# A gated mix of two linear-attention layers on one core: the first weights loaded by column groups on one queue, and a new order of the same operations

## The chip, the cores and the metric

One core of one Trainium2 chip runs the whole kernel. The metric is device time in microseconds of one execution. The kernel before was run three times; beside these one execution was taken with the hardware profiler, and all rows come from that one.

## The reference

The input x has 2048 tokens of 640 features; there are 32 heads of 20 features. Two attentions read the same x and are mixed by a gate per token.

```python
g = sigmoid((x * gate_w).sum(-1, keepdims=True))
# A: linear attention with softmax features
q, k, v = split(x @ wqkv)
phi(t) = concat(softmax(t @ w_phi), softmax(-(t @ w_phi)))       # 20 + 20 features
o_A = (phi(q) @ (phi(k).T @ v)) / (phi(q) @ phi(k).sum(tokens) + 1e-6)
# B: four segments of 512 tokens
p = softmax(q k.T / sqrt(20) + causal mask)                      # in the segment
a_mem = phi2(q) @ M / (phi2(q) @ z + 1e-6)                       # M, z: sums over the segments before
o_B = sigmoid(beta) * a_mem + (1 - sigmoid(beta)) * (p @ v)
out = g * (o_A @ wo_A) + (1 - g) * (o_B @ wo_B)
```

phi2(t) is t + 1 where t > 0 and exp(t) elsewhere. All tensors are bf16.

## The kernel before, in words

The program is a graph of 1317 operations. The functions of class GatedMix make them, in order of definition; three tables at the end of the file then say everything about their order. ORDER lists the operations' numbers in one sequence, and each engine executes its own operations in that sequence; ENGINE picks an engine for each operation that can run on more than one (an eviction from PSUM on ScalarE or VectorE, an elementwise step on VectorE or GpSimd); PLACE picks the PSUM banks and SBUF slots. The three came from a search outside the file, on a model of the chip. Semaphore waits follow from the reads and writes that each operation declares (emit, from L156 on). An engine is in order: an operation that waits holds all behind it, and this holds for SP's list of DMAs too.

The stages, by function:

- setup (L400): loads, weight layouts and masks. x is loaded as xT, features on partitions, by four transposing DMAs, x0 to x3, of 512 tokens each (L382). B's q and k weights are loaded into the staging tiles stq and stk (800 KB each, L386) and copied from there into WB (L439), where each head's 20 columns lie at a partition group of 32: for each of five column chunks c and for q and k, WB0 copies 80 columns and WB1 48. A's w_phi is folded into A's q and k weights (fuse, L500) from the transposed weights wkT and wqT; that gives WkA and WqA. "warm" is twelve matmuls on zeros (L427).
- b_proj(n) (L509) for each segment n: ten projections qkproj (five chunks by q and k; five matmuls of 512 columns each, L516); an eviction qk_ev for each chunk; four DMAs relw that write the rows 20 to 31 of each partition group to DRAM and four DMAs relr that read them back as head groups 5 to 7 of tile qk (numbered relr#0 to #15 over the segments); four value projections vproj (ten matmuls of 320 or 321 columns, L536 and L537; column 640 is the gate, loaded by GpSimd's DMA gw) with their eviction.
- b_pair (L644): scores of head groups. Three bursts per group (QKn.j#i, L628), each followed by two exps on ScalarE (L639) and a mask on GpSimd (L641); then PV (L673), and its division on VectorE (L680, L684).
- b_mem and b_ret: the memory. k is transposed by DMA (ktr), phi2 is applied, the sums M are kept; b_ret reads the memory for a segment (matmuls mr, L604, then mre, mrr, mrm on VectorE, L610 to L612).
- a_k(t) for each of 16 token tiles: pkA and vA (ten matmuls of 320 columns each, L702), two exps, sums and normalization (Anorm). a_kv sums phi(k) v in PSUM (kv) and phi(k) over tokens in tile acc by 64 adds, the "chain" (L763), which VectorE and GpSimd share: adds of one half follow one another whichever engine has them.
- a_fin: the matmuls zmm on acc (L775) and the scaled tile KV1, which all of A's outputs need.
- a_q(S) for each segment: pqA (L806), exps, ssum, whose result goes through DRAM by four DMAs rw (640 runs of 256 bytes each) and one DMA rd; then U (L851).
- final(t): out tiles, twenty matmuls of 320 columns each (L878), eviction and store.

The head before, in the order of each queue. SP: x1, WvA, x0, wkT, x3, wqT. ScalarE: the loads WvB, stq, stk, then its copies. GpSimd: gw, beta, wphi, then masks and copies. TensorE: warm, two value projections, qkproj0#0 and #1, one value projection, a first burst, then value projections, fuses and token projections mixed with the other eight qkproj0, of which the last, #9, stands 44th in TensorE's list. Around the second half, SP's list reads rw#0 to rw#3, relr#11, A_wo, relr#9, rd#0, and TensorE's burst QK2.2#2, which needs relr#8 to #11, follows.

Of the kernel before, what the change touches and what calls it, by code (L numbers as in the profile page):

```python
# [13 lines left out]
D = 640  # L14
# [3 lines left out]
NCH = 5  # L18
# [226 lines left out]
class GatedMix(Graph):  # L245
# [154 lines left out]
    def setup(self):  # L400
        ins, op = self.ins, self.op
        x2d = ins["A_x"].rearrange("b s d -> (b s) d")
        wqkv = ins["A_wqkv"]
        wsrc = lambda w: w.rearrange("(c p) n -> p c n", p=128)
        xT = self.xT
        self.dma("sp", "x0", xT[:, :, 0:LSEG], x2d[0:LSEG, :], W=[(xT, 0)], transpose=True)
        self.dma("act", "stq", self.stq[:, :, :], wsrc(ins["B_wq"]), W=[(self.stq, "*")])
        self.dma("act", "stk", self.stk[:, :, :], wsrc(ins["B_wk"]), W=[(self.stk, "*")])
        self.dma("act", "WvB", self.WvB[:, :, 0:D], wsrc(ins["B_wv"]), W=[(self.WvB, "w")])
# [21 lines left out]
        for c in range(NCH):  # L431
            for w in range(2):
                Wv = lambda w=w, c=c: self.WB[:, w, :, 128 * c:128 * (c + 1)].rearrange("p k (b r) -> p k b r", r=32)
                for part, (c0, n, r0, r1) in enumerate(((80 * c, 80, 0, DH), (400 + 48 * c, 48, DH, 32))):
                    o = op(("dve", "act", "pool"), f"WB{part}", None, R=[(st[w], "*")], W=[(self.WB, (w, c, part))])

                    def fn(e, o=o, Wv=Wv, w=w, c0=c0, n=n, r0=r0, r1=r1):
                        a, b = Wv()[:, :, :, r0:r1], st[w][:, :, c0:c0 + n].rearrange("p k (b r) -> p k b r", r=r1 - r0)
                        return e.activation(a, b, ACT.Copy) if o.stream == "act" else e.tensor_copy(a, b)  # L439
                    o.fn = fn  # L440
# [512 lines left out]
"""  # L953
ENGINE = "".join("""
210002211012121211121101010000110110101011110111101110011110111100011011000111011111111001010000111010101000001101011101011100010101101111110010001011
00100000101011111000110100101001100000001111000000001101011110101111111111100111000110001111111000
""".split())
PLACE = """
# [64 lines left out]
```

## Time and profile before

| | us |
|---|---|
| three runs | 339.05, 339.27, 341.5 |
| median | 339.27 |
| the profiled execution, its own time | 338.27 |
| its span, first to last instruction | 336.2 |
| TensorE's mean granted clock in it | 0.949 of full |

The profiled execution's own time is 2.07 longer than its span. Engines are named in the rows as PE (TensorE's matmuls), PEld (its weight loads), DVE (VectorE), ACT (ScalarE), POOL (GpSimd) and SP; a q behind the name (SPq) is that engine's issuing of DMAs. In a timeline a row gives start, duration, engine, line, operation, out<-in, count, and in brackets the idle time before it with what ended that. A row with xN is a run of N instructions of one form.

### The profile page before, as it was taken

The numbers are of one execution on the slowest core, as the hardware profiler recorded it, in microseconds if no ns is written. First come the engines' busy times: TensorE is split into PE (matmuls) and PEld (weight loads), VectorE is DVE, ScalarE is ACT, GpSimd is POOL, SyncE is SP. The second block draws the span as 40 slices with busy tenths as digits, with TensorE's granted clock in tenths as the row PEclk, the third lists the DMA queues.
The fourth block names the chain that finished last, engine by engine and source line by source line (L and its number), as shares of the span: only waits on it lengthen the run. The fifth ranks groups of instructions, "written<-read, shape, count | busy, mean of one in ns | idle before, by whom it ended". The sixth has DMA issues, their size and how long they took to land.

```text
span 336.2 us, 8681 instructions
## 1 busy us (share of the span) xinstructions
PE 298.2 (89%) x3726; PEld 188.0 (56%) x3726; DVE 243.9 (73%) x400; ACT 238.6 (71%) x276; POOL 196.8 (59%) x191
## 2 busy tenths in 40 slices
PE   4279999989899798998999698699989899799996
PEld 1136755655546665667576363346466667467874
DVE  3144778689999879988989986658486794554661
ACT  1228888878779679988879285688987876676402
POOL 6132147668899579998999781550445915514260
PEclk9789999999899899999999597869999999899999
DMA  8995005514201462024003313603479537612363
GB/s 196 272 238 120 0 2 86 95 41 91 20 2 31 76 100 60 16 18 67 16 2 99 75 23 95 189 3 81 94 188 186 110 80 134 173 55 69 80 99 117
DMA packets 68901, 29.42 MB, mean 88 GB/s; under 512 B 57952, under 2 KB 66944, under 8 KB 68864
## 3 DMA queue, kind: packets, MB, share of 16 engines
q1 hardware_dynamic: 66800, 26.39, 36.8%
q10 hardware_dynamic: 1968, 2.46, 2.6%
q8 instruction: 29, 0.48, 0.6%
q0 software_dynamic: 96, 0.04, 0.3%
q14 instruction: 8, 0.07, 0.1%
HBM read 9.54 MB, written 7.21 MB: 50 GB/s over the span
## 4 chain that ended last, share of the span: by engine, by line
PE 51%; DVE 23%; DMA 10%; ACT 4%; issue 4%; SPq 4%; POOL 3%; ACTq 0%; DVEq 0%; POOLq 0%
PE ps L878 9%; PE ps L516 8%; PE ps L702 7%; PE ps L806 6%; PE ps L673 6%; DVE acc L763 5%; PE ps L628 4%; DMA xT<-in_A_x_dram 4%; PE ps L851 3%; DVE E L724 2%; SPq L386 2%; DMA qk<-scr 2%; ACT exA L639 2%; SPq L382 2%; POOL acc L763 2%
## 5 line engine op out<-in xcount | busy, mean ns | idle before, releaser
L639 ACT ACTIVATE exA<-ps 128x1024 bf16<-128x1024 f32 x128 | 124.3, 1024 | 30.8 <-PE ps L628 30.2
L641 POOL TENSOR_SCALAR_AFFINE_SELECT exA<-exA 128x1024 bf16<-128x1024 bf16 (+1 forms) x64 | 60.3, 950 | 74.2 <-ACT exA L639 73.2
L763 POOL TENSOR_TENSOR acc<-acc,E 64x640 bf16<-64x640 bf16 x29 | 46.3, 1600 | 10.4 <-DMA acc<-acc 5.3
L516 PE MATMUL ps<-xT,WB 128*128 128x512 bf16 x200 | 50.3, 392 | 0.4 <-DVE qk L395 0.4
L628 PE MATMUL ps<-qk 20*128 20x384 bf16 (+3 forms) x512 | 32.8, 309 | 12.9 <-DVE aM L612 3.8
L673 PEld LDWEIGHTS ps<-v1B,exA 128*128 128x128 bf16 x1024 | 35.8, 96 | 5.5 <-issue 1.3
L673 PE MATMUL ps<-v1B,exA 128*128 128x21 bf16 x1024 | 37.2, 173 | 1.3 <-POOL exA L641 0.6
L639 ACT ACTIVATE exC<-ps 128x1024 bf16<-128x1024 f32 x32 | 31.3, 1025 | 8.8 <-PE ps L628 8.8
L516 PEld LDWEIGHTS ps<-xT,WB 128*128 128x128 bf16 x200 | 18.5, 101 | 23.2 <-issue 5.8
L536 PE MATMUL ps<-WvB,xT 128*128 128x320 bf16 x80 | 23.5, 311 | 8.3 <-DMA xT<-in_A_x_dram 8.1
L641 POOL TENSOR_SCALAR_AFFINE_SELECT exC<-exC 128x1024 bf16<-128x1024 bf16 x16 | 19.8, 1238 | 15.0 <-ACT exC L639 14.9
L763 DVE TENSOR_TENSOR acc<-acc,E 64x640 bf16<-64x640 bf16 x33 | 27.6, 846 | 0.9 <-POOL acc L763 0.2
L724 POOL TENSOR_TENSOR E<-E,z 128x640 bf16<-128x640 bf16 x20 | 26.1, 1314 | 3.1 <-DVE z L722 2.7
L806 PE MATMUL ps<-xT,WqA 128*128 128x512 bf16 x100 | 27.7, 424 | 0.2 <-ACT exC L639 0.2
L878 PE MATMUL ps<-Wo,oTA 128*128 128x320 bf16 x160 | 25.5, 310 | 2.1 <-DVE out L395 2.1
L628 PEld LDWEIGHTS ps<-qk 20*128 20x128 bf16 x512 | 9.2, 92 | 32.1 <-issue 12.4
L702 PE MATMUL ps<-WkA,xT 128*128 128x320 bf16 x160 | 25.7, 310 | 1.5 <-DVE qk L395 1.5
L813 ACT ACTIVATE ET<-ps 128x1024 bf16<-128x1024 f32 (+1 forms) x24 | 20.8, 883 | 7.1 <-PE ps L806 5.7
L714 ACT ACTIVATE E<-ps 128x640 bf16<-128x640 f32 x32 | 22.6, 709 | 4.2 <-PE ps L702 3.8
L673 PE MATMUL ps<-v1B,exC 128*128 128x21 bf16 x256 | 24.9, 172 | 0.0
L702 PE MATMUL ps<-WvA,xT 128*128 128x320 bf16 x160 | 24.3, 299 | 0.5 <-ACT exA L639 0.5
L720 DVE TENSOR_REDUCE z<-E 128x64 f32<-128x1280 bf16 x16 | 23.5, 1469 | 1.5 <-ACT E L714 1.5
(115 smaller groups left out, 549.6 us busy)
## 6 DMA issues: line engine op xcount, KB each, us to landing
scq<-rr SPq DMA_DIRECT2D x16, 160.0 KB
sp<-scq SPq DMA_DIRECT2D x4, 640.0 KB, 5.1
out_dram<-out SPq DMA_DIRECT2D x16, 160.0 KB, 3.7
scr<-qk SPq DMA_DIRECT2D x16, 120.0 KB
qk<-scr SPq DMA_DIRECT2D x16, 120.0 KB
WvB<-in_B_wv_dram ACTq DMA_DIRECT2D x1, 800.0 KB, 4.8
stq<-in_B_wq_dram ACTq DMA_DIRECT2D x1, 800.0 KB, 11.0
stk<-in_B_wk_dram ACTq DMA_DIRECT2D x1, 800.0 KB, 13.1
```

The source lines that it names most:

```text
L516: r = e.matmul(self.pf(pt, w, 0, LSEG), lhsT=WB[:, w, kc, 128 * c:128 * (c + 1)], rhs=xT[:, kc, LSEG * n:LSEG * (n + 1)], start=(kc == 0), ...
L536: e.matmul(self.pf(pt, 0, 0, 320), lhsT=l, rhs=self.WvB[:, kc, 0:320], start=(kc == 0), stop=(kc == 4))
L628: r = e.matmul(self.pf(pts[i // 2], i % 2, c0, N), lhsT=qk[32 * i:32 * i + DH, g, 1, 128 * j:128 * (j + 1)], rhs=qk[32 * i:32 * i + DH, g, ...
L639: self.op("act", "exp", lambda e, p=p: e.activation(view(p), self.pbanks(pts[p], 512), ACT.Exp, scale=scale), W=[(pts[p], 0), (t, (key, p))])
L641: self.op("pool", "mask" + str(len(pat)), lambda e: e.affine_select(mv(), mv(), pattern=pat, compare_op=ALU.is_ge, fill=0.0, base=0, chann ...
L673: r = e.matmul(self.pf(pt, 0, 84 * q + 21 * i, 21), lhsT=src(j, i, q), rhs=vt[:, j, head_of(g, i), :], start=(j == 0), stop=(j == q), skip ...
L702: r = e.matmul(self.pf(pt, b, 0, 320), lhsT=l, rhs=W[:, kc, 320 * b:320 * b + 320], start=(kc == 0), stop=(kc == 4))
L720: self.op("dve", "Zred", lambda e: e.tensor_reduce(z[:, :, :].rearrange("p s h -> p (s h)"), E[:, :, :].rearrange("p s (h d) -> p (s h) d" ...
L724: self.op(("pool", "dve"), "Anorm", lambda e, s=s: e.tensor_tensor(Ev(s), Ev(s), z[:, s, :].rearrange("p (h o) -> p h o", o=1).to_broadcas ...
L763: self.op(("dve", "pool"), "chain", lambda e, src=src, s=s, lo=lo: e.tensor_tensor(acc[lo:lo + 64, s, :], acc[lo:lo + 64, s, :], src(), AL ...
L806: r = e.matmul(self.pf(pt, k, 0, LSEG), lhsT=self.WqA[:, kc, 128 * c:128 * (c + 1)], rhs=xT[:, kc, LSEG * S:LSEG * (S + 1)], start=(kc == ...
L878: r = e.matmul(self.pf(pt, b, 0, 320), lhsT=oT[:, c, :], rhs=self.Wo[:, NCH * k + c, 320 * b:320 * b + 320], start=(first and c == 0), sto ...
```

## The change

Three things change.

1. The loads of the head. stq and stk are no longer loaded whole by ScalarE but by SP, in twelve pieces right after x0, in the order q then k, for column groups (chunk 0), (chunks 1, 2), (chunks 3, 4); each group has two pieces, the 80-column and the 48-column part of its chunks, so runs of 160 and 96 bytes for the first group and of 320 and 192 bytes for the others, 640 runs in each piece. WvB is loaded by SP too. A copy into WB now waits for its own piece alone.

```diff
-        self.dma("act", "stq", self.stq[:, :, :], wsrc(ins["B_wq"]), W=[(self.stq, "*")])
-        self.dma("act", "stk", self.stk[:, :, :], wsrc(ins["B_wk"]), W=[(self.stk, "*")])
-        self.dma("act", "WvB", self.WvB[:, :, 0:D], wsrc(ins["B_wv"]), W=[(self.WvB, "w")])
+        for l, (a, b) in enumerate(((0, 1), (1, 3), (3, NCH))):
+            for nm, st in (("B_wq", self.stq), ("B_wk", self.stk)):
+                for k, c0, c1 in ((0, 80 * a, 80 * b), (1, 400 + 48 * a, 400 + 48 * b)):
+                    self.dma("sp", f"st{k}", st[:, :, c0:c1], wsrc(ins[nm])[:, :, c0:c1], W=[(st, (k, l))], noncontig=True)
+        self.dma("sp", "WvB", self.WvB[:, :, 0:D], wsrc(ins["B_wv"]), W=[(self.WvB, "w")])
...
-                    o = op(("dve", "act", "pool"), f"WB{part}", None, R=[(st[w], "*")], W=[(self.WB, (w, c, part))])
+                    o = op(("dve", "act", "pool"), f"WB{part}", None, R=[(st[w], (part, (c + 1) // 2))], W=[(self.WB, (w, c, part))])
```

2. ORDER and PLACE are new throughout (1327 operations; the others are the same ones). The head by queue, read from the new ORDER. SP: x0, the twelve pieces, wkT, WvB, then segment 0's relw#1 and relw#0, WvA, wqT, x1, a ktr, the other relw, relr. GpSimd: six small masks and the loads wphi and beta among them, then masks and four of WB's copies, then gw. TensorE: warm, qkproj0 #0, #1, #2, #5, #3, #4, #8, a burst, qkproj0 #9, #7, the five fuses of WkA, qkproj0#6, a burst, pkA, a burst, the first value projection, then token and value projections mixed with bursts. Later, SP's list reads relr#11, relr#10, A_wo, two ktr, relr#8, rw#3, relr#9, rw#2, rw#1, rw#0, rd#0. Between ssum#0 and QK2.2#2 TensorE has five pqA projections, two mr, three bursts, two PV, a value projection and ssum#1 (before: two qkproj, three value projections, four bursts and a PV).

3. ENGINE is new. Operations per engine, before and after:

| operation | ScalarE | VectorE | GpSimd |
|---|---|---|---|
| chain and its first copy | | 33, 48 | 31, 16 |
| value eviction of B (v_ev) | 7, 0 | 9, 16 | |
| qk eviction | 6, 11 | 14, 9 | |
| Anorm | | 12, 13 | 20, 19 |
| memory added to the output (aMadd) | | 3, 5 | 9, 7 |
| scaling by rd's result (Esc1, Esc2) | | 6, 3 | 6, 9 |
| scaling of U's reciprocal | 2, 7 | 14, 9 | |
| copies into WB | 9, 5 | 4, 11 | 7, 4 |
| fuse eviction | 6, 4 | 4, 6 | |
| vA and out evictions | 16, 14 | 16, 18 | |
| first kv eviction, K1, Mz1, zero fill of qk | 2, 1 | 5, 7 | 4, 3 |

## Rows read from the trace of the kernel before

**Rows 1.** The page: busy time of the engines; TensorE's strip in 40 slices.
```profile
PE 298.2 (89%) x3726; PEld 188.0 (56%) x3726; DVE 243.9 (73%) x400; ACT 238.6 (71%) x276; POOL 196.8 (59%) x191
...
PE   4279999989899798998999698699989899799996
```

**Rows 2.** Windows: length, then busy us (instructions) of each engine, clock, DMA share, GB/s.
```profile
0.00:26.00 26.00, 13.26 (x59) 6.17 (x60) 8.65 (x31) 5.40 (x10) 10.63 (x37) 0.87 1.01 235
26.00:80.00 54.00, 52.93 (x570) 31.86 (x568) 40.74 (x66) 45.96 (x60) 27.26 (x27) 1.00 0.29 57
80.00:205.00 125.00, 112.90 (x1476) 72.22 (x1475) 114.73 (x167) 100.16 (x114) 104.57 (x80) 0.94 0.24 44
205.00:230.00 25.00, 21.51 (x192) 11.01 (x191) 14.95 (x28) 17.41 (x18) 10.71 (x9) 0.83 0.41 110
```

**Rows 3.** Timeline of SP: issues of DMAs in the head and in three later places.
```profile
0.81 4.85 SPq L382 DMA_TRANSPOSE xT<-in_A_x_dram  x1
...
6.60 11.09 SPq L382 DMA_TRANSPOSE xT<-in_A_x_dram  x1
...
24.46 3.73 SPq L382 DMA_TRANSPOSE wqT<-in_A_wqkv_dram  x1
...
178.69 0.41 SPq L386 DMA_DIRECT2D Wo<-in_B_wo_dram  x1
...
237.06 2.68 SPq L386 DMA_DIRECT2D scq<-rr  x4
241.87 0.40 SPq L386 DMA_DIRECT2D sp<-scq  x1
```

**Rows 4.** Timeline of TensorE: the head, and around the stall at 216 us.
```profile
4.69 4.65 PE L427 MATMUL ps<-zero 128*128 128x512 bf16 x12 [4.69 <-DVE zero L421]
...
15.36 0.42 PE L536 MATMUL ps<-WvB,xT 128*128 128x320 bf16 x1 [6.01 <-DMA xT<-in_A_x_dram]
...
21.62 2.32 PE L516 MATMUL ps<-xT,WB 128*128 128x512 bf16 x10
...
26.98 1.52 PE L702 MATMUL ps<-WvA,xT 128*128 128x320 bf16 x10
...
29.73 0.79 PE L500 MATMUL ps<-BD,wkT 128*128 128x140 bf16 x12
...
215.98 0.40 PE L628 MATMUL ps<-qk 20*128 20x256 bf16 x8 [2.97 <-DMA qk<-scr]
...
218.42 2.31 PE L806 MATMUL ps<-xT,WqA 128*128 128x512 bf16 x5 [0.21 <-ACT exC L639]
```

**Rows 5.** Timeline of ScalarE: the first exp.
```profile
25.71 1.02 ACT L639 ACTIVATE exA<-ps 128x1024 bf16<-128x1024 f32 x1 [0.70 <-PE ps L628]
```

**Rows 6.** DMA: the queue's packets from 18 to 22 us; issues, us to landing.
```profile
q1 hardware_dynamic: 3794, 0.96, 106.1%
...
wphi<-in_A_w_phi_dram POOLq DMA_DIRECT2D x1, 25.0 KB, 8.5
WvB<-in_gate_w_dram POOLq DMA_DIRECT2D x1, 1.2 KB, 9.3
...
wqT<-in_A_wqkv_dram SPq DMA_TRANSPOSE x1, 5.7
```

**Rows 7.** Chain of waits in order of time, 196 to 224 us: start, us, what.
```profile
196.70 0.35 PE ps L775 x10
...
209.15 6.79 DMA qk<-scr
```

**Rows 8.** Groups of instructions by line and form: busy us, mean ns | idle before.
```profile
L763 POOL TENSOR_TENSOR acc<-acc,E 64x640 bf16<-64x640 bf16 x29 | 46.3, 1600 | 10.4 <-DMA acc<-acc 5.3 <-DVE E L724 3.0
...
L763 DVE TENSOR_TENSOR acc<-acc,E 64x640 bf16<-64x640 bf16 x33 | 27.6, 846 | 0.9 <-POOL acc L763 0.2
...
L395 DVE CAST qk<-ps 128x1024 bf16<-128x1024 f32 x14 | 17.1, 1219 | 10.3 <-PE ps L516 10.3
...
L395 DVE CAST v1B<-ps 128x640 bf16<-128x640 f32 x9 | 7.4, 827 | 0.3
```

More of the change, by code (lines that the diff above doesn't have):

```diff
@@ L915 @@
 ORDER = """
[37 rows of a table removed]
[37 rows of a table added]
 """
 ENGINE = "".join("""
-210002211012121211121101010000110110101011110111101110011110111100011011000111011111111001010000111010101000001101011101011100010101101111110010001011
-00100000101011111000110100101001100000001111000000001101011110101111111111100111000110001111111000
+002000100101021100221010011011010001011111011101111111010010010111110111011000111101111100001010011101010011000000000001011110010010001100100000001100
+00100001000000110000110101111000001100000000111100001011111101001001110011011111001111001101110001
 """.split())
 PLACE = """
[11 rows of a table removed]
[11 rows of a table added]
 """
```

96 rows, old and new, of tables (ORDER, PLACE) are left out of this document.

## The prediction, made before the changed kernel was run

> **What bounds the kernel now.** I read the page first, then the windows by stage, then SP's and TensorE's timelines of the head, then the chain of waits. On the page TensorE is the busiest engine, busy 89% of the span, and its strip shows where the rest is: three weak slices at the head (4, 2, 7, then 9s) and dents between two thirds and three quarters of the way (6, 8, 6) [rows 1]. The windows say the same in us: until 26 us TensorE is busy 13.26 of 26.00, from 26 to 80 us 52.93 of 54.00, so there it is the bound; from 80 to 205 us VectorE is busy 114.73 of 125.00 and TensorE 112.90, so those two share the limit; from 205 to 230 us neither is full and the clock is 0.83 [rows 2].
>
> The head is bound by loads. SP first issues x1 and WvA, then x0, whose issue alone takes 11.09 us because ACT's three 800 KB loads fill the DMA engines [rows 3]. The warm-up matmuls begin at 4.69 us and last 4.65. The first real matmul starts at 15.36, having waited 6.01 us for xT; the first q and k projections start at 21.62 [rows 4]; the first exp starts at 25.71 [rows 5]. ScalarE needs q and k before it has an exp to do, and q and k come late.
>
> **The change part by part.** I count TensorE's work at the full-clock pace: ten matmuls of 512 columns (two q or k projections) 2.16, from the chain's pace of the 2.32 row less its tail; a token projection (ten of 320 columns) 1.52 with its tail, 1.39 without; a fuse (six matmuls) half of a 0.79 row less tail, 0.31 [rows 4].
>
> *Head loads.* x0 goes first; it starts at 0.81 like x1 before, so SP is free at 5.7 at the latest (4.85 of issue beside three loads; 3.73 for a transpose with little beside it). It lands about 5.7 us after its issue begins, as wqT did [rows 3, 6], at 6.5. Then SP issues twelve pieces. Each has 640 runs, as have the four scq writes whose issue took 2.68 together, 0.67 each; 0.41 for one Wo load, 640 runs too, is the lower end [rows 3]. At 0.67 the last piece is issued at 5.7 + 8.0 = 13.7. A piece lands about 2.1 us after its issue: the read that waited for those four writes went out at 241.87, 2.13 after the last issue ended at 239.74 [rows 3]. The upper end is wphi, 640 short runs, 8.5 us after its issue [rows 6]. Runs as short as 96 to 320 bytes from DRAM don't stand in this trace; the nearest are the transposes' 253-byte packets (3794 for 0.96 MB in 4 us with all engines full), 16.9 ns per packet and engine [rows 6]. At that price 7680 packets on 16 engines take 8.1 us, no more than their issue.
>
> So q's first group (pieces 1 and 2) is there at 5.7 + 1.3 + 2.1 = 9.1, its two copies, a quarter us each by my estimate from the other short copies, end at 9.6, and TensorE starts real work at 9.7 instead of 15.36, 0.4 us after the warm-up ends. Five matmuls took 2.31 at the half level (1.2 GHz) [rows 4]; the clock hadn't risen at 15.36, since a matmul of 320 columns took 0.42, so I take the first two projections at the half level: 4.6, and the other eight 8.6. The later pieces arrive at 10.4, 11.8, 13.1, 14.5 and 15.8 by twos, each ahead of its projection. Two bursts (0.7) and five fuses (1.6) stand among them; wkT, issued at 13.7, lands at 19.4, before its first fuse. In all 9.7 + 15.5 = 25.2. By then TensorE has done 10.8 + 0.7 + 1.6 = 13.1 us of full-clock work. Before, by 25.2 it had done three value projections and two q/k projections: 3 x 1.39 + 2.2 = 6.4. Gain 6.7 us. From there both kernels give TensorE work without a gap, as 26 to 80 us shows for the one before [rows 2]. Ends: with 8.5 us landing everything is 6.4 later and the gain 0.3; with 0.41 per issue and the full clock at once it is about 9.7. I take 6.7, by the nearest rows.
>
> WvB, which ACT issued first thing, now stands behind wkT on SP: issued at 13.7 + 3.7 = 17.4 with its 0.8 MB. Its first use stands behind a token projection and a burst after the 25.2 above, at 27; it costs nothing while these cover it, and wkT's 5.7 would put its landing at 23. GpSimd issues the gate column (gw, the same first use) behind its last weight copy, which waits for piece 12: issued at about 17, and with the 9.3 us that it took before [rows 6], landed at 26.5. That cover is the thinnest; each us past 27 would be a us of the gain. WvA, wqT, x1 now stand behind segment 0's first two relw, which wait for the last qk eviction (some 27 us); with at most 3.7 each to issue and 5.7 to land they are there by 40, and their first uses are 12 token projections' worth of TensorE work later (after 42). No cost; each of them has that cover.
>
> *SP around segment 2's last relr.* Before, QK2.2#2 (segment 2's first burst of a pair that needs relr) waits for relr#9, which SP reaches only behind four rw, relr#11 and A_wo; the chain has 6.79 us of DMA here [rows 7], TensorE is idle 2.97 at 215.98, and two projections behind it run at the half level, at 2.31 each instead of half of that [rows 4], 2.97 + 2.31 = 5.3 in all. Now relr#9 is behind a single rw and the load of A_wo was issued before; between that rw's release (ssum#0) and the burst stand 10.6 us of TensorE work where 8.9 stood. The wait should go. What is late next is the memory read's VectorE chain, which also holds TensorE here. So 0 to 5.3; I take half, 2.6.
>
> *Engines.* VectorE gets 13 of the chain's adds (0.846 each, 11.0), 7 value evictions (0.827, 5.8), and gives up 5 qk evictions (1.219, 6.1) [rows 8]; the dozen other moves, at one to three operations each, I estimate at 3 more. So VectorE +13.7, GpSimd -13 x 1.6 = -20.8 and a little [rows 8], ScalarE about -3. Most of the adds fall before zmm (at 196.7 [rows 7]), in the stretch where VectorE has 125.00 - 114.73 = 10.3 us free [rows 2]; with the 6.7 us that the head gives, 17 us are there for some 12. The ends are 0 and +13.7; I take +2, near the free time's end, since GpSimd's slow adds, after which VectorE's adds of the same chain waited, go too.
>
> *The rest of the order* is permuted everywhere. No row prices that; its bounds are 12.1 us either way, what TensorE idles from 80 to 205 us (125.00 - 112.90 [rows 2]). I take 0.
>
> Sum: -6.7 - 2.6 + 2.0 = -7.3 on the profiled execution's 338.27: 331.0. That execution is 1.0 under the median of the three runs, 0.3%, less than any term's error; I give 331 for the median too.
>
> **The rivals.**
> 1. *More than the head.* The stall at 216 goes wholly and a third of TensorE's 12.1 idle us between 80 and 205 with it, without a charge for VectorE: -6.7 - 5.3 - 4.0, 322.3. For it: these losses stand in the old order, not in the operations. Against: in an in-order kernel the next late thing takes most of such a gain. 0.11.
> 2. *The head's gain is absorbed.* TensorE is 6.7 us ahead at 25 us, but VectorE, nearly full from 80 us on, reaches zmm no sooner than at 196.7: 338. For it: VectorE's 114.73 of 125.00 [rows 2]. Against: TensorE's 52.93 of 54.00 before it, so an early head moves that whole stretch. 0.17.
> 3. *VectorE becomes the bound, slower.* If it stays at its 92% share with 12 us more before zmm, that stretch takes 12 / 0.92 = 13 longer; less the head's 6.7, +6.3: 345. It decides from the point where zmm comes later than 196.7 + 1. Against: the chain's next operand comes from VectorE itself, so its share can rise. 0.09.
> 4. *The pieces land one after another.* If each piece is issued and landed before the next is served, 0.67 + 2.13 = 2.8 each, the seventh and eighth arrive at 28 and the last at 39; ten projections end near 41 with 13.1 us of work done, where before 22 were done: 9 us lost, 347. Against it: four such DMAs took 4.81 from first issue to the read behind them, not 11.2 [rows 3]. 0.08.
>
> The Trainium skill speaks for the fourth: "DMA: Bandwidth & Descriptors", section "Anatomy of one DMA", gives a fixed cost of about 2 us per DMA plus bytes at 436 GB/s, measured on GpSimd's queue. By it, were the twelve served in turn, they would take 12 x 2.0 + 3.8 = 27.8 us, an estimate, and the last would land near 33. The four writes' 4.81 us [rows 3] say that most of that cost overlaps.
>
> **How the numbers follow.** The forecast has 0.55, the rivals 0.11, 0.17, 0.09 and 0.08. About 1% (3.4 us) is what a measurement of this kernel can tell from no change. Faster by over 1%: forecast and rival 1, 0.66. Within 1%: rival 2, 0.17. Slower: rivals 3 and 4, 0.17. The range runs from rival 1's 322 to 341, past rival 2; it leaves out rivals 3 and 4 and little else.
>
> **What would show it.** Right: first TensorE work at about 9.7 us, first exp near 20 instead of 25.71; TensorE busy over 16 of the first 26 us; SP's pieces 0.6 to 0.8 us apart; no DMA wait before QK2.2#2; zmm at 188 to 192. Wrong: last piece landing after 20 us; zmm at 196 or later with VectorE over 95%; GpSimd idle while VectorE's chain is what the end waits for.

## The result, and the profile after

The changed kernel took 327.71 us (median of 4 runs, 327.3 to 329.87), the kernel before 339.16 beside it (4 runs): ratio 0.9669, 95% interval 0.9599 to 0.9739. Forecast was 331.0 in a range of 322 to 341. The profiled execution has a span of 326.3 us where the one before had 336.2: 9.9 us less. A second set of runs of the same kernel gave 329.25 (6 runs, ratio 0.9669 again, 0.9627 to 0.9711), so the experiments below are set against both medians. One execution of all those reported here, a fourth of the kernel with the new loads under the old order, was slow (369.08 us at a mean granted clock of 0.75) and is left out of that kernel's numbers.

The page, busy time and TensorE's strip, answering to [rows 1]:

```profile
PE 294.8 (90%) x3726; PEld 186.1 (57%) x3726; DVE 243.4 (75%) x425; ACT 236.2 (72%) x270; POOL 173.7 (53%) x172
...
PE   5999999989989599896898769989899999999995
```

The three weak slices at the head (4, 2, 7) are one (5, then 9s). TensorE's sum fell by 3.4 us, so most of the 9.9 is idle time that went. GpSimd lost 23.1 us, and VectorE, which got 25 instructions more, is at 243.4 where it was at 243.9.

The windows, answering to [rows 2], with the same columns:

```profile
0.00:26.00 26.00, 21.56 (x122) 9.37 (x122) 9.97 (x40) 12.08 (x18) 10.98 (x36) 0.93 0.78 153
26.00:80.00 54.00, 51.56 (x664) 32.23 (x664) 48.40 (x79) 47.71 (x56) 30.17 (x28) 1.00 0.45 79
80.00:205.00 125.00, 106.96 (x1329) 67.07 (x1328) 112.72 (x173) 92.58 (x105) 75.48 (x60) 0.93 0.29 59
205.00:230.00 25.00, 23.70 (x400) 15.35 (x398) 19.15 (x37) 21.70 (x25) 14.36 (x12) 1.00 0.61 127
```

In the first 26 us TensorE is busy 21.56 instead of 13.26. From 205 to 230 us the clock is 1.00 instead of 0.83. From 80 to 205 us TensorE is busy 106.96 where it was 112.90, so it idles 18.0 us instead of 12.1: part of what the head won is lost here (below).

SP's timeline of the head, answering to [rows 3]:

```profile
0.81 2.86 SPq L382 DMA_TRANSPOSE xT<-in_A_x_dram  x1
3.73 1.13 SPq L385 DMA_DIRECT2D stq<-in_B_wq_dram  x2
4.91 1.76 SPq L385 DMA_DIRECT2D stk<-in_B_wk_dram  x2
...
10.23 1.18 SPq L385 DMA_DIRECT2D stk<-in_B_wk_dram  x2
11.45 4.16 SPq L382 DMA_TRANSPOSE wkT<-in_A_wqkv_dram  x1
15.65 0.58 SPq L386 DMA_DIRECT2D WvB<-in_B_wv_dram  x1
```

x0 takes 2.86 us to issue, not 4.85, and the twelve pieces go out from 3.73 to 11.41, most of them 0.55 to 0.6 apart. TensorE's timeline, answering to [rows 4], and ScalarE's first exp, answering to [rows 5]:

```profile
1.33 4.53 PE L429 MATMUL ps<-zero 128*128 128x512 bf16 x12 [1.33 <-DVE Mk L448]
7.97 5.10 PE L518 MATMUL ps<-xT,WB 128*128 128x512 bf16 x15 [2.11 <-DVE WB L441]
13.49 4.48 PE L518 MATMUL ps<-xT,WB 128*128 128x512 bf16 x20 [0.42 <-ACT WB L441]
...
211.60 0.40 PE L630 MATMUL ps<-qk 20*128 20x256 bf16 x8
211.93 1.25 PE L518 MATMUL ps<-xT,WB 128*128 128x512 bf16 x5
```

```profile
18.51 1.94 ACT L641 ACTIVATE exA<-ps 128x1024 bf16<-128x1024 f32 x2
```

Real work starts at 7.97 instead of 15.36, and the first exp at 18.51 instead of 25.71. At 211.60 stands QK2.2#2, before at 215.98 behind a wait of 2.97: it waits for nothing now, and the projection behind it takes 1.25 for five matmuls, the full clock, where the two behind it took 2.31 each. The zmm, at 196.70 in [rows 7]:

```profile
189.08 0.41 PE L777 MATMUL ps<-onec,acc 64*128 64x1 bf16 x10 [3.36 <-DVE acc L765]
```

It comes 7.6 us earlier, but not because TensorE is that far ahead. Two windows from the start to the zmm, the kernel before and then the changed one, with the columns of [rows 2]:

```profile
0.00:196.70 196.70, 171.90 (x1972) 105.89 (x1973) 156.47 (x243) 145.02 (x174) 139.12 (x140) 0.95 0.37 75
```

```profile
0.00:189.08 189.08, 166.70 (x1878) 100.50 (x1879) 157.24 (x261) 138.52 (x160) 111.23 (x119) 0.96 0.40 76
```

The new order has 94 fewer matmuls ahead of its zmm, 5.2 us of busy time; only 2.4 of the 7.6 us are idle time saved (24.8 against 22.4). The groups, answering to [rows 8]:

```profile
L765 DVE TENSOR_TENSOR acc<-acc,E 64x640 bf16<-64x640 bf16 x46 | 38.5, 845 | 2.2 <-DMA acc<-acc 1.2
...
L765 POOL TENSOR_TENSOR acc<-acc,E 64x640 bf16<-64x640 bf16 x16 | 23.6, 1476 | 16.3 <-DMA acc<-acc 7.5 <-DVE acc L765 4.4 <-DVE E L726 3.9
```

### The profile page after: what moved, and what is told of

It is laid out like the page before. It is cut to its first block, busy times and chain, and to the rows that moved or that the text cites. A ratio compares the mean times of both kernels' runs of the same rounds, so it can differ in the third digit from the quotient of the medians.

```text
span 326.3 us, 8697 instructions
## 1 busy us (share of the span) xinstructions
PE 294.8 (90%) x3726; PEld 186.1 (57%) x3726; DVE 243.4 (75%) x425; ACT 236.2 (72%) x270; POOL 173.7 (53%) x172
## 4 chain that ended last, share of the span: by engine, by line
PE 51%; DVE 29%; DMA 5%; SPq 4%; ACT 4%; POOL 4%; issue 3%
PE ps L880 11%; DVE acc L765 9%; PE ps L675 7%; PE ps L518 6%; PE ps L808 6%; PE ps L630 5%; PE ps L704 4%; SPq L382 4%; PE ps L853 3%; DVE z L722 3%; PE ps L743 2%; DVE E L726 2%; PE ps L538 2%; ACT exA L641 2%; DMA xT<-in_A_x_dram 2%
## 5 line engine op out<-in xcount | busy, mean ns | idle before, releaser
L643 POOL TENSOR_SCALAR_AFFINE_SELECT exA<-exA 128x512 bf16<-128x512 bf16 (+1 forms) x64 | 61.4, 966 | 73.4 <-ACT exA L641 73.2
L630 PE MATMUL ps<-qk 20*128 20x256 bf16 (+3 forms) x512 | 32.7, 309 | 9.9 <-DVE v1B L395 3.0
L765 DVE TENSOR_TENSOR acc<-acc,E 64x640 bf16<-64x640 bf16 x46 | 38.5, 845 | 2.2 <-DMA acc<-acc 1.2
L765 POOL TENSOR_TENSOR acc<-acc,E 64x640 bf16<-64x640 bf16 x16 | 23.6, 1476 | 16.3 <-DMA acc<-acc 7.5
L808 PE MATMUL ps<-xT,WqA 128*128 128x512 bf16 x100 | 26.1, 404 | 0.8 <-DVE oB L686 0.8
L630 PEld LDWEIGHTS ps<-qk 20*128 20x128 bf16 x512 | 9.2, 92 | 29.5 <-issue 13.7
L880 PE MATMUL ps<-Wo,oTA 128*128 128x320 bf16 x160 | 24.3, 300 | 0.2 <-DMA oTA<-oA 0.2
L643 POOL TENSOR_SCALAR_AFFINE_SELECT exC<-exC 128x1024 bf16<-128x1024 bf16 x16 | 18.9, 1181 | 9.8 <-ACT exC L641 9.6
L880 PE MATMUL ps<-Wo,oTB 128*128 128x320 bf16 x160 | 24.0, 299 | 0.0
```

Source lines behind the costliest of these rows:

```text
L630: r = e.matmul(self.pf(pts[i // 2], i % 2, c0, N), lhsT=qk[32 * i:32 * i + DH, g, 1, 128 * j:128 * (j + 1)], rhs=qk[32 * i:32 * i + DH, g, ...
L643: self.op("pool", "mask" + str(len(pat)), lambda e: e.affine_select(mv(), mv(), pattern=pat, compare_op=ALU.is_ge, fill=0.0, base=0, chann ...
L765: self.op(("dve", "pool"), "chain", lambda e, src=src, s=s, lo=lo: e.tensor_tensor(acc[lo:lo + 64, s, :], acc[lo:lo + 64, s, :], src(), AL ...
L808: r = e.matmul(self.pf(pt, k, 0, LSEG), lhsT=self.WqA[:, kc, 128 * c:128 * (c + 1)], rhs=xT[:, kc, LSEG * S:LSEG * (S + 1)], start=(kc == ...
L880: r = e.matmul(self.pf(pt, b, 0, 320), lhsT=oT[:, c, :], rhs=self.Wo[:, NCH * k + c, 320 * b:320 * b + 320], start=(first and c == 0), sto ...
```

## The experiments

All kernels but one (the new loads under the old order) are the changed one with one edit, of which the lines that matter are shown. Differences are given against 327.71 and 329.25 in turn. The theory: the head's time comes from x0 going first and from column groups, and carries through; the relr stall is a term of its own; the moved adds cost or gain little.

**Whole tiles instead of column groups.** Two loads on SP take the place of the twelve, and each copy into WB waits for its whole tile.

```diff
...
-                    self.dma("sp", f"st{k}", st[:, :, c0:c1], wsrc(ins[nm])[:, :, c0:c1], W=[(st, (k, l))], noncontig=True)
+        self.dma("sp", "stq", self.stq[:, :, :], wsrc(ins["B_wq"]), W=[(self.stq, "*")])
+        self.dma("sp", "stk", self.stk[:, :, :], wsrc(ins["B_wk"]), W=[(self.stk, "*")])
...
```

> The changed kernel, but q's and k's weights come as two whole tiles on SP (x0, q, k, wkT, WvB) and each copy waits for its whole tile. Theory (one queue in order of need gives the head its gain; the column groups only matter if whole tiles arrive later than TensorE can use them): 1.64 MB in long rows needs about 4.5 us at 370 GB/s against about 8 us for the pieces, so q whole lands near 8 us, k near 10.5, first projection at 8 to 9 us instead of 7.97, and SP is free for wkT some 6 us earlier: within 1 us of the changed kernel, 327 to 329. Rival (the column groups are what gives the gain): first projection 3 us or more later, 331 or more.

Measured: 332.76, 5.1 or 3.5 slower (ratio to before 0.9828, 0.9754 to 0.9902). TensorE's timeline of it:

```profile
11.08 11.17 PE L516 MATMUL ps<-xT,WB 128*128 128x512 bf16 x35 [4.45 <-DVE WB L439]
```

The first projection waits for all of wq and starts 3.1 us later. The theory that one long load would do as well was wrong: with this list of SP the groups win, although two whole tiles need far fewer issues. Not all of the 3.1 us need be the tile's length, though: with only two loads ahead of it, wkT is issued from 4.95 us on, beside the two tiles (11.45 in the changed kernel), while the DMA engines are full (a share of 1.14 from 4 to 12 us). No run has whole tiles with a later wkT.

**The old loads under the new order.** ScalarE issues stq, stk and WvB whole, as before; the order and the engines are the new ones, and each copy into WB waits for its whole tile.

```diff
...
-                    self.dma("sp", f"st{k}", st[:, :, c0:c1], wsrc(ins[nm])[:, :, c0:c1], W=[(st, (k, l))], noncontig=True)
-        self.dma("sp", "WvB", self.WvB[:, :, 0:D], wsrc(ins["B_wv"]), W=[(self.WvB, "w")])
+        self.dma("act", "stq", self.stq[:, :, :], wsrc(ins["B_wq"]), W=[(self.stq, "*")])
+        self.dma("act", "stk", self.stk[:, :, :], wsrc(ins["B_wk"]), W=[(self.stk, "*")])
+        self.dma("act", "WvB", self.WvB[:, :, 0:D], wsrc(ins["B_wv"]), W=[(self.WvB, "w")])
...
```

> The changed kernel, but the three head loads are issued by ScalarE as before (WvB, q, k whole) beside SP's x0. Theory (the head's gain comes from loading on one queue in order of need, so that x0 and q don't share the DMA engines with what is needed later): first projection at 12 to 14 us, first exp 4 to 5 us later than in the changed kernel, and the whole 4 to 5 us longer, about 332. Rival (the new order of TensorE's work, projections first, is the gain, whoever loads): within 1.5 us of the changed kernel.

Measured: 336.96 (10 runs), 9.3 or 7.7 slower; ratio to before 0.9956 (0.991 to 1.0002). Its timeline:

```profile
13.68 5.77 PE L516 MATMUL ps<-xT,WB 128*128 128x512 bf16 x15 [7.86 <-DMA xT<-in_A_x_dram]
```

x0, beside three large loads, lands so late that TensorE starts at 13.68. The new order and engines without their loads are worth almost nothing.

**A later head.** wkT and WvB go ahead of x0 in SP's list; nothing else moves.

```diff
+    order = [17, 13] + [a for a in order if a not in (17, 13)]
```

> The changed kernel, but wkT and WvB (1.64 MB) are issued on SP ahead of x0 and the pieces, so that the first projection comes about 5 us later and nothing else changes. Theory (a head that is ahead moves the whole kernel): the end comes later by the same 4 to 5 us, about 332. Rival (the head's gain is absorbed, because VectorE is nearly full from 80 us to zmm): zmm moves by less than 2 us and the end by less than 2 us, 328 to 329.5.

Measured: 335.18, 7.5 or 5.9 slower (0.99, 0.9822 to 0.9977). TensorE's timeline, at the head and at 77 us:

```profile
13.43 3.74 PE L518 MATMUL ps<-xT,WB 128*128 128x512 bf16 x10 [7.01 <-DVE WB L441]
...
77.53 3.79 PE L518 MATMUL ps<-xT,WB 128*128 128x512 bf16 x9 [0.19 <-issue]
...
195.49 0.40 PE L777 MATMUL ps<-onec,acc 64*128 64x1 bf16 x10 [3.36 <-DVE acc L765]
```

The head starts 5.5 us late and zmm is 6.4 late: nothing downstream absorbs a late head in this order. The part above 5.5 is the clock. Against the first profile of the changed kernel the lag is 5.4 until 75 us and 7.1 after nine matmuls at 77.53 that ran at the half level (1.2 GHz), behind a TensorE idle of 0.84; in that first profile ten matmuls behind the same idle took 2.33:

```profile
69.64 0.49 PE L502 MATMUL ps<-BD,wqT 128*128 128x140 bf16 x6 [0.84 <-DVE qk L395]
...
71.86 2.33 PE L518 MATMUL ps<-xT,WB 128*128 128x512 bf16 x10
```

In the second profile of the same, unchanged kernel they took 4.02, at a granted clock of 0.58 (1.00 in the first):

```profile
69.09 0.49 PE L502 MATMUL ps<-BD,wqT 128*128 128x140 bf16 x6 [0.83 <-DVE qk L395]
...
71.31 4.02 PE L518 MATMUL ps<-xT,WB 128*128 128x512 bf16 x10
...
189.45 0.40 PE L777 MATMUL ps<-onec,acc 64*128 64x1 bf16 x10 [3.36 <-DVE acc L765]
```

So whether the clock falls there differs from execution to execution, and it is worth some 1.7 us. Against that second profile zmm is 6.0 late for a head that starts 5.5 late (13.43 against 7.89).

**Pieces, but copies that wait for the whole tile.** Each copy into WB waits for all six pieces of its tile; SP's list stays as it is.

```diff
-                    o = op(("dve", "act", "pool"), f"WB{part}", None, R=[(st[w], (part, (c + 1) // 2))], W=[(self.WB, (w, c, part))])
+                    o = op(("dve", "act", "pool"), f"WB{part}", None, R=[(st[w], (q, l)) for q in range(2) for l in range(3)], W=[(self.WB, (w, c, part))])
...
```

> The changed kernel with its twelve pieces, but every copy into WB waits for all six pieces of its tile, so the groups are loaded and not used. Theory (the grouping pays because TensorE can start on the first group): the first projection starts at 13 to 14 us, when q's last piece lands, 5 to 6 us later than in the changed kernel, and, with the 1.4 us at the end for each us at the head that the late-head run showed, the end is 7 to 9 us later, 335 to 337. Rival (grouping doesn't matter, only the queue's order does): within 1.5 us of the changed kernel.

Measured: 335.19, 7.5 or 5.9 slower (0.9876, 0.9812 to 0.994).

```profile
13.68 4.72 PE L518 MATMUL ps<-xT,WB 128*128 128x512 bf16 x15 [7.24 <-DVE WB L441]
```

The pieces alone lose against two whole tiles (13.68 against 11.08): what cutting gains, it gains because each copy waits for its piece alone.

**The new loads under the old order.** This is the kernel before, its order and engines, with the change's loads; SP issues x1, WvB, x0 and then the pieces. Against the kernel before, beside the loads themselves:

```diff
-    k.replay([int(w) for w in ORDER.split()], [int(w) for w in ENGINE], place)
+    order = [a + 10 if a > 2 else a for a in map(int, ORDER.split()) if a not in (1, 2)]
+    head = [18, 13, 0] + list(range(1, 13))
+    k.replay(head + [a for a in order if a not in head], [int(w) for w in ENGINE], place)
```

> The kernel before with its own order and engines, but with the head's loads all on SP: x1, WvB, x0, the twelve pieces, WvA, wkT and on; each copy waits for its own piece. Theory (the loads are what was won in the head, and a head that is ahead moves any order): the first value projection starts near 9 us instead of 15.36, the first exp near 17 instead of 25.71, the end 5 to 9 us earlier than before, 331 to 335. Rival (only the new order can use the early weights, the old one was searched for late ones): within 2 us of the kernel before.

Measured: 340.4 (median of three runs, 337 to 341.9), ratio to before 1.0014 (0.9922 to 1.0107): no gain. TensorE's timeline:

```profile
10.63 0.30 PE L538 MATMUL ps<-WvB,xT 128*128 128x320 bf16 x1 [1.57 <-issue]
...
20.49 4.45 PE L518 MATMUL ps<-xT,WB 128*128 128x512 bf16 x10 [6.09 <-ACT WB L441]
```

The old order begins with value projections, so x1, WvB and x0 come ahead of the pieces, and the pieces go out from 10.81 on. The first q and k projections start at 20.49, behind an idle of 6.09, and run at the half level; they started at 21.62 before. The first value projection did come earlier (10.63 for 15.36), but TensorE was busy 12.98 of the first 26 us, where it was 13.26 before: in the one arrangement that was tried, the loads give the old order no lead at all. So this run says that they don't pay alone; what a lead would be worth under the old order it doesn't say.

**The relr behind the writes again.** relr#11, A_wo and relr#9 stand behind the four rw, as in the kernel before.

```diff
+    late = [500, 1093, 498]
+    order = [a for a in order if a not in late]
+    i = order.index(1109) + 1
+    k.replay(order[:i] + late + order[i:], [int(w) for w in ENGINE], place)
```

> The changed kernel, but on SP relr#11, the load of A_wo and relr#9 stand behind segment 0's four rw again, as in the kernel before. Forecast's term (the wait before the first burst that needs relr#8 to #11 is worth 0 to 5.3 us, half taken): the burst waits 1 to 4 us for qk from DRAM near 212 us and the end comes 1 to 4 us later, 329 to 332. Rival (TensorE's longer row of work between ssum#0 and that burst covers it, whatever SP's order): no wait, within 1 us of the changed kernel.

Measured: 333.29 (329.77 to 334.4), 5.6 or 4.0 slower (0.9806, 0.9729 to 0.9883).

```profile
216.13 0.61 PE L630 MATMUL ps<-qk 20*128 20x256 bf16 x8 [2.31 <-DMA qk<-scr]
217.07 1.91 PE L518 MATMUL ps<-xT,WB 128*128 128x512 bf16 x4 [0.33 <-issue]
```

The wait is back, 2.31 us of the 2.97 before, and the half clock behind it. zmm came at 190.7, so 1.6 of the loss (1.3 against the second profile) arose ahead of the stall, though nothing there was edited; the other 2.7 to 4.0 us came with the stall.

**x1, WvA and wqT right behind WvB.**

```diff
+    early = [18, 21, 22]
+    order = [a for a in order if a not in early]
+    i = order.index(13) + 1
+    k.replay(order[:i] + early + order[i:], [int(w) for w in ENGINE], place)
```

> The changed kernel, but SP issues x1, WvA and wqT right behind WvB at 16 us, where it is idle until 25.9, and not behind the first two relw. Theory (these three loads are on the chain of waits from 26.6 to 42 us in the changed kernel, though TensorE is busy for all but 2.4 of the 54 us after 26): 0.5 to 2 us faster, 326 to 327. Rival (they have cover, as forecast, and now stand in front of relw and relr, which the segment's second half needs): no change within 1 us or slower by up to 2.

Measured: 327.63 (6 runs, 326.31 to 329.06), ratio 0.9656 (0.9603 to 0.9709): no change. The cover that the forecast gave these late loads was there.

**The chain's adds on the engines of before** (33 on VectorE, 29 on GpSimd, the same adds as before on each).

```diff
-            o.stream = o.engs[e]
+            o.stream = o.engs[int(next(chain)) if o.name == "chain" else e]
```

> The changed kernel with the engines of the 62 chain adds as before the change (33 on VectorE and 29 on GpSimd, not 46 and 16); the sequence is the same. Theory of the forecast (VectorE's extra adds mostly fit its free time and cost about 2 us): 1 to 3 us faster, about 326. Second theory (the moved adds help, since GpSimd's add takes nearly twice as long and the chain's adds follow one another): 2 to 8 us slower, zmm later by as much. No change within 1 us would say that neither engine's share decides.

Measured: 335.03, 7.3 or 5.8 slower (0.9875, 0.9794 to 0.9956), with the same head. Two views show it, TensorE's timeline and, for the second row, GpSimd's:

```profile
71.29 0.49 PE L503 MATMUL ps<-BD,wqT 128*128 128x140 bf16 x6 [3.24 <-DVE qk L396]
...
119.99 0.55 PE L676 MATMUL ps<-v1B,exA 128*128 128x21 bf16 x14 [7.09 <-POOL exC L644]
...
196.74 0.42 PE L778 MATMUL ps<-onec,acc 64*128 64x1 bf16 x10 [6.94 <-DVE acc L766]
```

```profile
107.86 2.03 POOL L766 TENSOR_TENSOR acc<-acc,E 64x640 bf16<-64x640 bf16 x1 [6.91 <-DVE acc L766]
110.65 1.39 POOL L766 TENSOR_TENSOR acc<-acc,E 64x640 bf16<-64x640 bf16 x1 [0.76 <-DVE E L727]
...
113.69 1.39 POOL L766 TENSOR_TENSOR acc<-acc,E 64x640 bf16<-64x640 bf16 x1
...
118.59 1.34 POOL L644 TENSOR_SCALAR_AFFINE_SELECT exC<-exC 128x1024 bf16<-128x1024 bf16 x1
```

GpSimd waits 6.91 us for VectorE's part of the chain, does three adds and the two normalizations and two masks between them, and only then the mask exC for which TensorE waits 7.09. That wait doesn't stand in the changed kernel; the waits at 71 and at zmm were 0.84 and 3.36 there. zmm is 7.7 late.

**All 62 adds on VectorE.**

```diff
-            o.stream = o.engs[e]
+            o.stream = "dve" if o.name == "chain" else o.engs[e]
```

> The changed kernel with all 62 chain adds on VectorE (46 there before this edit, 16 on GpSimd). Theory after the chain-engine run (what counts is how long the chain's adds take one after another, 0.85 us on VectorE against about 1.5 on GpSimd, not VectorE's sum): 0 to 4 us faster, 324 to 328, and zmm earlier than 189.1 by as much. Rival (VectorE, busy 99.8 of the 110 us before zmm, is the bound from here on; it gets 16 x 0.85 = 13.5 us more): 3 to 10 us slower, 331 to 338, zmm at 193 or later, VectorE's share over 95%.

Measured: 334.7 (6 runs, 333.4 to 336.69), ratio 0.9839 (0.9796 to 0.9881), 5.5 above the 329.25 measured beside it.

```profile
L765 DVE TENSOR_TENSOR acc<-acc,E 64x640 bf16<-64x640 bf16 x62 | 41.7, 681 | 4.6 <-DMA acc<-acc 3.2
```

```profile
69.84 0.49 PE L502 MATMUL ps<-BD,wqT 128*128 128x140 bf16 x6 [1.29 <-DVE qk L395]
...
72.26 3.58 PE L518 MATMUL ps<-xT,WB 128*128 128x512 bf16 x10
...
165.33 0.56 PE L606 MATMUL ps<-Mz,pq 128*128 128x84 bf16 x10 [1.59 <-DVE oB L686]
...
196.37 0.42 PE L777 MATMUL ps<-onec,acc 64*128 64x1 bf16 x10 [5.93 <-DVE acc L765]
```

VectorE's adds took 41.7 us in sum, only 3.2 more than the 46 of the changed kernel. So it is not their sum that costs. They stand in VectorE's queue ahead of what TensorE waits for: the waits for qk, oB and the last add grew from 0.84, 0.85 and 3.36 to 1.29, 1.59 and 5.93, and zmm is 7.3 late (6.9 against the second profile). These three are 3.8 us of the 7.3; 1.9 more are matmuls that ran longer, such as the ten at 72.26 (3.58 for 2.33), and the rest isn't traced. VectorE isn't full: from 80 to 196 us it is busy 101.02 of 116.00. So the rival's sign was right and its reason, an engine without free time, was not.

**The changed kernel again,** with no edit, beside the run of all adds on VectorE.

> The changed kernel once more, unchanged, beside the run with all chain adds on VectorE, so that the two are compared on one chip: 327 to 329.

Measured: 329.25, as said above. No experiment gave a kernel that is faster than the changed one beyond this spread.

## Why the prediction was right, and where it was not

**The head (-6.7): right up to 26 us, a little small; what becomes of it is not as said.** Every step came out as said, each somewhat early: x0's issue 2.86 instead of 4.85, pieces at 0.55 to 0.6 instead of 0.67, so real work at 7.97 instead of 9.7, the first exp at 18.51 instead of about 20, TensorE busy 21.56 of 26 (over 16 was expected). The late-head kernel shows that in the new order a shift of the head reaches the end: 5.5 us at the head, 6.0 to 6.4 at zmm, 5.9 to 7.5 in the time. Against the kernel before, the lead does not simply last. TensorE's idle time by stretch (length less busy, from the windows and the page):

| stretch, us | before | after |
|---|---|---|
| 0 to 26 | 12.7 | 4.4 |
| 26 to 80 | 1.1 | 2.4 |
| 80 to 205 | 12.1 | 18.0 |
| 205 to 230 | 3.5 | 1.3 |
| 230 to the end | 8.6 | 5.3 |

By 205 us the idle sums are 25.9 and 24.9: of the 8.3 us won in the head 1.0 is left. The final gain is made up behind 205 us (5.5) and by a shorter busy time of the same matmuls (3.4). The zmm at 189.08, inside the 188 to 192 that was to show the forecast right, is no proof of the lead, since the new order has 5.2 us less of TensorE's work ahead of it. Part of the step is the loads, part the grouping: with whole tiles 3.5 to 5.1 of the time are lost again, with pieces that are waited for together 5.9 to 7.5.

**The late loads (0): right.** Moving x1, WvA and wqT forward changed nothing.

**The stall at segment 2's relr (-2.6): right in mechanism, short in size.** Half of 5.3 was taken for fear that VectorE would hold TensorE there next. It didn't: the burst runs without a wait. Putting the stall back costs 4.0 to 5.6, of which 2.7 to 4.0 came with it. Two reasons were given, SP's order and more TensorE work between the writes and the burst. The second isn't enough: with that work in place and SP's old order 2.31 us of wait return. SP's order removes the stall.

**The engines (+2): wrong, and the step that failed.** The step is the charge for "VectorE +13.7". Its count was right: at the mean times of before, the new engines' instructions add 14.2 (adds 27.6 to 38.5 us, +10.9 for 11.0; 16 value evictions for 9, +5.8; qk evictions -6.1; GpSimd -23.1 for -20.8 and a little). But many of VectorE's instructions ran shorter, 11.8 us in sum, and its busy time went from 243.9 to 243.4. Two such groups of the changed kernel, with the same counts before, where they took 1316 and 678 ns each:

```profile
L557 DVE TENSOR_SCALAR kt<-kt 128x2560 bf16<-128x2560 bf16 x3 | 2.5, 818 | 0.0
...
L481 DVE TENSOR_TENSOR Mm<-Mg,eb 128x80 bf16<-128x80 bf16 x5 | 1.6, 339 | 0.0
```

The chain's adds show what the length hangs on. In every one of these traces a VectorE add during which GpSimd executes nothing takes at most 490 ns (9 of the 33 before, 18 of the 46 after, 36 of the 62 with all adds on VectorE), and the others take about 1 us on average, beside GpSimd's adds and multiplications as well as beside its masks. The means over all adds are 846 before, 845 after, 681 with no add on GpSimd and 937 with 29 adds there under the new order. The number of adds on GpSimd alone doesn't set them, since 29 gave 846 under the old order; what is at work beside each add does. The Trainium skill says why this can be: "GPSIMD Engine Reference", section "1. Specifications", has the two engines share their SBUF interfaces, with contention when a VectorE instruction is in a 2-port performance mode or has two SBUF inputs. The adds and the second group above, with two inputs each, agree with it; the first group has one input, and no run here shows its mode.

And the price of an add isn't its busy time but what stands behind it in its queue. With 29 adds on GpSimd that was, among others, a mask and 7.09 us of TensorE. Both ways away from 46 and 16 cost under the new order: +5.8 to +7.3 with 29 adds on GpSimd, +5.5 with none. So under this order the moved adds are worth 5.8 to 7.3 us, where the forecast charged 2 for the engines; the other engine moves, and the adds under the old order, were not tried alone.

A charge by VectorE is there even so, in waits. From 80 to 205 us TensorE waits 9.3 us for VectorE before and 16.2 after (sums of the waits' rows; 17.6 in the second profile). The longest before and then after, with us in total, times, and the longest one:

```profile
PE ps L628 <- DVE aM L612: 3.8, 2, 2.6
PE ps L628 <- DVE Mm L479: 1.9, 1, 1.9
```

```profile
PE ps L777 <- DVE acc L765: 3.4, 1, 3.4
PE ps L630 <- DVE v1B L395: 3.0, 1, 3.0
PE ps L630 <- DVE vA L395: 2.6, 1, 2.6
```

Of the three after, the first is for the chain's last add, the second for a value eviction, of which VectorE has seven more. Which of these waits the new engines make, and which the new order, no run separates.

**The sum.** Each part that was taken out costs 3.5 to 9.3 us, and together these come to more than the 9.9 us that went. They aren't additive: taking one out of this order hurts the rest too. The runs with one half alone say so best (loads alone, in the arrangement tried, 1.0014; order and engines alone 0.9956; together 0.9669). So the forecast landed near in part by luck. From 26 to 205 us, where it had +2 for the engines and 0 for the rest of the order, TensorE's idle time grew by 7.3; behind 205 us, where it had -2.6, it shrank by 5.5, and 3.4 more went because the same 3726 matmuls were busy for a shorter time. These errors partly cancel. What the rest of the order is worth by itself stays open.

**The rivals.** Absorbed (zmm not before 196.7): by its sign no, 189.08; but most of the head's lead over the kernel before is spent by 205 us, much of it in waits for VectorE, so the rival had hold of something real. VectorE as the bound: no, the time fell and VectorE's busy time didn't grow; still, one sign of being wrong, VectorE's chain being what TensorE waits for, shows at zmm with 3.36 us (no wait there before), and the all-VectorE kernel shows a loss from the same side, by the queue and not by its sum. Pieces served one after another: no. The last piece's issue ends at 11.41, and 20 matmuls of the first projections run from 13.49 to 17.97 at 0.22 each, with no wait between; the fixed cost of about 2 us per DMA that "DMA: Bandwidth & Descriptors" in the Trainium skill gives (section "Anatomy of one DMA", measured there on GpSimd's queue) overlaps here, as the four writes had said. By it twelve in turn would take 24 us, an estimate; here they were issued, landed and used within 14.3. More than the head (322.3): not reached in the time. The stall did go wholly and VectorE's busy time took no charge, but of the idle time between 80 and 205 us no third went: it grew by 5.9.

## What to carry to other kernels

Where the first operations wait for a weight, load what the first one needs first, alone in its queue, and let each consumer wait for its own piece; then order the work to use it; here neither half paid without the other. Price an operation that changes its engine by what is queued behind it there, and by who waits for that, before its busy time. Follow a lead to the end, by idle time stretch by stretch: here 8.3 us won at the head were 1.0 by 205 us. One instruction that comes earlier doesn't show the lead when the order has moved work past it.

## What the runs showed that was not expected

- Twelve loads of 640 short runs (96 to 320 bytes) each beat two whole tiles by 3.5 to 5.1 us, though they move more slowly: 170 GB/s from 4 to 8 us and 218 from 8 to 12, where the kernel with whole tiles moved 262 from 4 to 12 (wkT, which it issues early, among that).
- The same kernel, behind the same idle of 0.83 to 0.84 us, ran its next ten matmuls once in 2.33 us and once in 4.02. One profile of an order with short idles can't price them to better than the some 1.7 us that the half level costs there.
- A chain add on VectorE takes at most 490 ns with nothing on GpSimd beside it, and about 1 us on average otherwise.
- The issue of one and the same kind of transpose holds SP for 2.86 us (x0), 4.16 (wkT) or 8.90 (wqT, issued behind the 0.8 MB of WvA).
